# Seven half-size products in place of eight in part of the first MLP layer, in the last two tiles of a retention and MLP kernel

## The chip, the cores and the metric

The kernel runs on one core of a Trainium2 chip. The metric is the device time of one execution in microseconds (us). The engines of the core are named as in the profile: PE (TensorE, matrix products), PEld (its weight loads), DVE (VectorE), ACT (ScalarE), POOL (GpSimd) and SP (SyncE, which here issues stores). Products land in PSUM, eight banks of 512 float32 values per partition; the other operands lie in SBUF.

## The reference

Inputs are `q`, `k`, `v` of shape 8 x 8 x 576 x 64 (batch, heads, positions, head size), two small matrices `U` (576 x 32) and `V` (32 x 576) and two weight matrices `w_ch1` (512 x 2048) and `w_ch2` (2048 x 512). All are float32.

```
scores = scale * (q @ k^T) * Dmat          # Dmat[i, j] = gamma_h ** (i - j) for i >= j, else 0
x      = heads side by side of (scores @ v)   # 8 x 576 x 512
u      = x + (x^T @ U @ V)^T
out    = u + max(u @ w_ch1, 0) @ w_ch2
```

The change concerns `max(u @ w_ch1, 0)`, the first layer of the MLP.

## The kernel before

The 8 x 576 = 4608 rows of `u` are worked on as nine MLP tiles of 512 rows (`NT = 9`, tiles 0 to 8). The attention of a later batch is interleaved with the MLP of an earlier tile; tiles 7 and 8 have no attention beside them, since there are only eight batches. All matrix operands are bfloat16, and PE accumulates in float32.

The rows of `u` lie in a ring of 16 chunks of 128 rows, `ring["u"]`, and turned, `ring["uT"]` (128 partitions of one quarter of the 512 columns, four quarters `cc` apart). `w1_sb` holds the first weight matrix in four blocks of 128 rows, `w2_sb` the second in 16 blocks.

**First layer.** The 2048 columns of `w_ch1` are 16 row blocks of 128 of the turned result. For one block, `first(f)` runs four matmuls of 128 x 128 weights against 512 moving columns, accumulated in one PSUM bank, and `relu(f)` on ACT writes the block to `y1` in SBUF as bfloat16. From tile 2 on the blocks go in the order 0, 8, 1, 9, 2, 10 and so on, a block of the upper half of `y1` and its partner of the lower half in turn. So four blocks in a row (2, 10, 3, 11, say) form a two-by-two arrangement of halves.

**Second layer.** From tile 2 on it already runs in seven products instead of eight: `product(n, half)` takes quarters of `y1` (two halves of rows, two halves of blocks) and of `w2`, or sums of such quarters, in a scheme in which seven products of half-size matrices replace eight. Its matmuls have 256 moving columns, 112 in a tile. The sums of `y1` are made by DVE: `sum_up(a, z)` writes two 128x512 sums after each pair of blocks of both halves (`GROUPS` says after which unit), and `difference` overwrites a quarter after the last block. The parts of the result go through `after_1` to `after_7`, on ACT, DVE and POOL, to `o_sb` and are stored by SP.

**Order.** The units of a tile are 16 of the first layer and 14 of the second. The program issues them one after the other, and every engine works on its own instructions in the order in which they were issued (`Pinned` keeps that order); between engines there are semaphores, made from which part of a tile an instruction reads and writes. PSUM banks come from three pools: three banks "mm" (`ps_mm`), which the blocks of the first layer and the products of the second take in turn, three banks "att" and one tile of two banks "pss", which the attention uses. In tiles 7 and 8 the last two pools lie idle but for two "att" banks at the very end of tile 8, where `rows_apart` keeps the last product's two halves apart so that the first can be stored sooner.

The loop over the tiles in the kernel before is `for j in range(1, NT)`; it issues a tile's units with the attention steps that are due between them. The buffers `k_sets`, `v_sets` (three of each) and `q_raw` (two) hold the inputs of the batches and are no longer read once the last batch's attention is over, which is during tile 6.

Of the kernel before, what the change touches and what calls it, by code (L numbers as in the profile page):

```python
# [8 lines left out]
FP32 = mybir.dt.float32  # L9
BF16 = mybir.dt.bfloat16  # L10
AF = mybir.ActivationFunctionType
ALU = mybir.AluOpType
# [55 lines left out]
def kernel(  # L68
# [12 lines left out]
    pe = Pinned(tc, nc.tensor)  # L81
    dve = Pinned(tc, nc.vector)
    act = Pinned(tc, nc.scalar)
# [6 lines left out]
    R = moe_U.shape[1]  # L90
    P = 128
# [4 lines left out]
    NF = dff // P  # L96
# [5 lines left out]
    NT = B * S // 512  # L102
# [19 lines left out]
    CH = 64  # L122
# [12 lines left out]
    ps_mm = ctx.enter_context(tc.tile_pool(name="ps_mm", bufs=3, space=bass.MemoryType.PSUM))  # L135
    banks = {}
# [6 lines left out]
    q_raw = [consts.tile([P, NR_COLS], BF16, name=f"q_all{i}") for i in range(NQ)]  # L143
# [61 lines left out]
    w1_sb = consts.tile([P, NCC, dff], BF16, name="w1_sb")  # L205
# [343 lines left out]
    def mix_turn_by_dma(a, n):  # L549
# [363 lines left out]

    GROUPS = {4: (0, 2), 8: (2, 4), 12: (4, 6), 15: (6, 8)}

    def sums_of_w2(part):

        f = slice(part * HF // 2, (part + 1) * HF // 2)
        (b11, b12), (b21, b22) = (
            [w2_sb[:, fh * HF:(fh + 1) * HF, q * HD:(q + 1) * HD][:, f, :] for q in range(2)]  # L920
            for fh in range(2)
        )
        t3, t2, t4 = (w2_sums[:, i, f, :] for i in range(3))
        for to, x, y, op in (
            (t3, b22, b12, ALU.subtract), (t2, t3, b11, ALU.add), (t4, b21, t2, ALU.subtract),
        ):
            dve.tensor_tensor(out=to, in0=x, in1=y, op=op)

    def last_sum_of_w2(part):
        f = slice(part * HF // 2, (part + 1) * HF // 2)  # L930
        x = w2_sb[:, 0:HF, HD:dm][:, f, :]
        dve.tensor_tensor(out=x, in0=x, in1=w2_sb[:, 0:HF, 0:HD][:, f, :], op=ALU.subtract)

    def mlp_units(j):
        held = {}
# [65 lines left out]
        def sum_up(a, z):  # L1001

            f = slice(a, z)
            s1, s2 = (y1_sums[:, i, f, :] for i in range(2))
            dve.tensor_tensor(
                out=s1, in0=quarter(1, 0)[:, f, :], in1=quarter(1, 1)[:, f, :], op=ALU.add
            )
            dve.tensor_tensor(out=s2, in0=s1, in1=quarter(0, 0)[:, f, :], op=ALU.subtract)

        def difference(a, z):  # L1010
            f = slice(a, z)
            x = quarter(1, 0)[:, f, :]
            dve.tensor_tensor(out=x, in0=quarter(0, 0)[:, f, :], in1=x, op=ALU.subtract)
# [78 lines left out]
        def product(n, half):  # L1092
            bank, fresh, left, right, after = products[n]
            if bank not in held and rows_apart(bank):
                held[bank] = [
                    banks["one"].tile([P, 2, HD], FP32, tag="att", name="ps_y2") for _ in range(2)
                ]
            if bank not in held:
                held[bank] = ps_mm.tile([P, 2, HD], FP32, tag="mm", name="ps_y2")
            apart = rows_apart(bank)  # L1100
            for f in range(HF):
                pe.matmul(
                    bank_rows(bank, half), left()[:, f, half * P:(half + 1) * P],
                    right()[:, f, :], start=(fresh and (apart or half == 0) and f == 0),
                    stop=(f == HF - 1), skip_group_check=True,
                )
            if j == NT - 1 and after is after_3:
                after_3_rows(half)
            elif half == 1 and after:
                after()  # L1110

        def unit(n, alone=True):

            i, part = divmod(n - NF, 4)
            if n < NF:
                first(order[n])
            elif sums:
                product(*divmod(n - NF, 2))
            else:
                second(i, part)  # L1120
            if alone and n < NF:
                relu(order[n])
                if sums and n in GROUPS:
# [7 lines left out]
        steps = {"y": ahead, "R": relu, "M": lambda n: unit(n, False), "O": add_and_store}  # L1131
        return [lambda n=n: unit(n) for n in range(NF + (14 if sums else 16))], steps


# [141 lines left out]
    for h in range(H):  # L1276
# [6 lines left out]
        out=ident, in_=ident, compare_op=ALU.not_equal, fill=1.0, base=0,  # L1283
# [13 lines left out]
    for i in range(2):  # L1297
# [7 lines left out]
        out=maskbin, in_=maskbin, compare_op=ALU.is_ge, fill=0.0, base=0,  # L1305
# [27 lines left out]
    for h in range(H):  # L1333
        dve.tensor_scalar(
            out=masks[:, h, :, :], in0=mask64, scalar1=float(gammas[h] ** -CH), scalar2=None,
            op0=ALU.mult,
# [6 lines left out]
            tc.tile_pool(name="ps_" + name, bufs=n, space=bass.MemoryType.PSUM))  # L1343


    for j in range(1, NT):
# [12 lines left out]
        if j == 2:  # L1359
            steps += [(at, 3, lambda i=i: last_sum_of_w2(i)) for i, at in enumerate((2, 3))]  # L1360
        if 1 < j and j + 2 < B:
            wait_for_turns(j)
            load_for_turns(j + 2)
            if j + 3 < B:
                clear_pads(j + 3)
        if j + 2 < B:
            at = 22 if j == 1 else 20
            steps += [(at + h, 4, lambda h=h: scale_head(j + 2, h)) for h in range(H)]
        steps.sort(key=lambda s: s[:2])
        for n, unit in enumerate(units1 if j == 1 else mlp_units(j)[0]):  # L1370
            while steps and steps[0][0] <= n:
                steps.pop(0)[2]()
            if j > 1 or n >= 3:
                unit()
        for s in steps:
            s[2]()

# [28 lines left out]
```

## Time and profile before

| what | value |
|---|---|
| time, three runs | 313.93, 315.33, 315.69 us, median 315.33 us |
| the profiled execution's own time | 315.51 us |
| span of the profiled execution | 313.8 us |
| PE busy | 305.6 us (97%) |
| DVE busy | 229.0 us (73%) |
| ACT busy | 166.8 us (53%) |
| POOL busy | 131.3 us (42%) |

The span runs from the first to the last instruction; the execution's own time is longer by what lies around it. A busy share is an average over stages. The part of the span that matters here is its last 56 us: tile 7's first layer from about 258 us, its second from about 272, tile 8's from about 284 and 298. Each row of a timeline has a start, a duration, the engine, the operation, its output and inputs, a shape and a count; in square brackets stands how long the engine had been idle before, and what ended that. PSUM tiles of both layers are called `ps_y`, the first layer's result `y_t`, the sums of it `y_sums`, the sums of `w2` `kv_runs`, the parts of the output `o_sb`.

### The profile page before, as it was taken

How to read it: one execution, taken by the hardware profiler on the slowest of the kernel's cores; microseconds unless marked ns; L12 is line 12 of the kernel's file. 1: busy time of each engine (PE TensorE's matmuls, PEld its weight loads, DVE VectorE, ACT ScalarE, POOL GpSimd, SP SyncE). 2: the span in 40 equal slices, each digit the busy share in tenths (PEclk: the TensorE clock that was granted, in tenths of full speed). 3: DMA queues.
4: the chain of work that ended last, by engine and by line, in shares of the span. 5: the costliest groups of instructions: out<-in, count | busy, mean ns of one | idle time of the engine just before them, and what ended most of it. 6: DMA issues, size and time to landing. Idle time of an engine off the chain costs nothing.

```text
span 313.8 us, 9434 instructions
## 1 busy us (share of the span) xinstructions
PE 305.6 (97%) x3937; PEld 190.9 (61%) x3952; DVE 229.0 (73%) x562; ACT 166.8 (53%) x346; POOL 131.3 (42%) x171
## 2 busy tenths in 40 slices
PE   8799999999999999999999999999999999999995
PEld 3575446745544557855784578457845784685484
DVE  6776818877988997899688968996799772352245
ACT  7556605447725775377437745774377406604610
POOL 8492258849302952259439612961200120040040
PEclk9979999999999999999999999999999999999999
DMA  7999999999995999799999994999910052002003
GB/s 117 193 182 198 204 212 145 170 184 133 173 123 162 158 113 146 118 157 148 154 210 162 143 148 119 178 139 118 212 56 4 3 131 86 2 33 102 0 2 135
DMA packets 154523, 40.58 MB, mean 129 GB/s; under 512 B 139088, under 2 KB 153456, under 8 KB 154480
## 3 DMA queue, kind: packets, MB, share of 16 engines
q0 software_dynamic: 91344, 17.09, 71.7%
q1 hardware_dynamic: 63136, 22.88, 40.9%
q8 instruction: 31, 0.51, 0.7%
q14 instruction: 12, 0.10, 0.1%
HBM read 36.85 MB, written 9.44 MB: 147 GB/s over the span
## 4 chain that ended last, share of the span: by engine, by line
PE 84%; DVE 7%; DMA 4%; issue 2%; SPq 1%; ACT 0%; POOL 0%; DVEq 0%; POOLq 0%
PE ps_y L25 69%; PE xh L25 5%; PE ps_b L25 4%; DMA given<-in_v_dram 2%; DMA kv_runs<-in_v_dram 2%; PE sc L25 2%; SPq L25 1%; PE pss L25 1%; DVE u_t L25 1%; PE ps_h L25 1%; PE ps_at L25 1%; DVE v_all L25 1%; DVE S L25 1%; DVE V_sb L25 1%; DVE qT_all L25 1%
## 5 line engine op out<-in xcount | busy, mean ns | idle before, releaser
L25 PE MATMUL ps_y<-uT_t,w_sb 128*128 128x512 bf16 x576 | 130.3, 379 | 0.2
L25 ACT ACTIVATE y_t<-ps_y 128x512 bf16<-128x512 f32 x144 | 85.6, 597 | 59.6 <-PE ps_y L25 58.5
L25 PEld LDWEIGHTS <-w_sb 128*128 128x128 bf16 x576 | 54.4, 98 | 61.5 <-issue 0.4
L25 POOL TENSOR_TENSOR o_sb<-o_sb,u_t 128x512 f32<-128x512 f32 x21 | 23.9, 1152 | 104.8 <-DVE o_sb L25 100.3
L25 PEld LDWEIGHTS <-y_t 128*128 128x128 bf16 x576 | 55.2, 98 | 18.9
L25 PE MATMUL ps_y<-w_sb,y_t 128*128 128x256 bf16 (+1 forms) x345 | 56.4, 310 | 0.5 <-issue 0.2
L25 DVE SCALAR_TENSOR_TENSOR S<-S,keep,pss 128x64 bf16<-128x64 bf16 x168 | 47.0, 280 | 6.0 <-ACT S L25 0.9
L25 DVE TENSOR_TENSOR o_sb<-ps_y,o_sb 128x512 f32<-128x512 f32 (+1 forms) x37 | 24.4, 662 | 26.6 <-PE ps_y L25 12.8
L25 DVE TENSOR_TENSOR ret<-sc,qsrow 128x640 bf16<-128x640 f32 x48 | 39.2, 819 | 2.5 <-PE sc L25 2.2
L25 PEld LDWEIGHTS <-y_sums 128*128 128x128 bf16 x336 | 32.0, 98 | 5.2 <-issue 0.5
L25 POOL DMA_DIRECT2D k_all<-in_k_dram x36 | 30.1, 853 | 8.2 <-DMA w_sb<-in_moe_w_ch_dram 8.2
L25 POOL DMA_DIRECT2D q_all<-in_q_dram x37 | 29.3, 801 | 5.5 <-DMA w_sb<-in_moe_w_ch_dram 4.2
L25 ACT ACTIVATE v_all<-v_all,vs 128x320 bf16<-128x320 bf16 x40 | 18.7, 548 | 22.1 <-DMA v_all<-in_v_dram 20.8
L25 DVE TENSOR_TENSOR y_sums<-y_t 128x512 bf16<-128x512 bf16 x28 | 11.8, 420 | 22.1 <-ACT y_t L25 22.1
L25 POOL DMA_DIRECT2D v_all<-in_v_dram x31 | 26.5, 918 | 2.4 <-DMA k_all<-in_k_dram 1.6
L25 PE MATMUL ps_y<-w_sb,y_sums 128*128 128x256 bf16 x224 | 27.4, 273 | 0.1
L25 PE MATMUL ps_y<-kv_runs,y_t 128*128 128x256 bf16 x224 | 26.9, 273 | 0.2
L25 ACT ACTIVATE x_t<-xh,xs 128x320 bf16<-128x320 f32 x48 | 22.7, 523 | 7.4 <-PE xh L25 5.8
L25 DVE TENSOR_TENSOR u_t<-ps_h,x_t 128x512 bf16<-128x512 f32 (+2 forms) x39 | 22.4, 629 | 2.5 <-PE ps_h L25 2.3
L25 POOL COPY landed<-uT_t 128x4 bf16<-128x4 bf16 (+3 forms) x5 | 0.9, 188 | 38.4 <-DMA uT_t<-u_t 38.4
L25 PE MATMUL ps_y<-kv_runs,y_sums 128*128 128x256 bf16 x112 | 14.1, 273 | 0.3 <-issue 0.3
L25 PEld LDWEIGHTS <-ret 128*128 128x128 bf16 (+1 forms) x320 | 11.8, 98 | 2.5 <-issue 0.2
(133 smaller groups left out, 297.0 us busy)
## 6 DMA issues: line engine op xcount, KB each, us to landing
out_dram<-o_sb SPq DMA_DIRECT2D x35, 256.0 KB, 2.6
w_sb<-in_moe_w_ch_dram POOLq DMA_DIRECT2D x8, 512.0 KB, 12.1
v_all<-in_v_dram POOLq DMA_DIRECT2D x25, 128.0 KB, 10.8
k_all<-in_k_dram POOLq DMA_DIRECT2D x24, 128.0 KB, 6.3
q_all<-in_q_dram POOLq DMA_DIRECT2D x20, 128.0 KB, 4.8
q_all<-in_q_dram POOLq DMA_DIRECT2D x12, 144.0 KB, 6.0
given<-in_v_dram SPq DMA_DIRECT2D x8, 128.0 KB, 5.5
kv_runs<-in_v_dram SPq DMA_DIRECT2D x3, 256.0 KB, 6.0
```

Source lines behind the costliest of these rows:

```text
L25: return self._tc.keep_in_program_order(call(*args, **kwargs))
```

## The change

The loop over tiles ends before tile 7, and a new function `last_tiles` issues tiles 7 and 8 with an order written out by hand.

In each, the first layer's four groups of four blocks are treated in two ways. The first (blocks 0, 8, 1, 9) and the last (6, 14, 7, 15) stay as they are. The second (group 1: blocks 2, 10, 3, 11) and the third (group 2: 4, 12, 5, 13) are computed in the same seven-product scheme as the second layer. The halves are those of the 512 columns of `u` that are summed over (`c` = 0, 1), of the blocks (lower, upper) and of the 512 rows of the tile (`t` = 0, 1). One product `seventh(n, g)` is four matmuls of 128 x 128 weights against 256 moving columns. Seven products make 28 such matmuls for a group, where the plain group has 16 of 512 columns.

The scheme needs four sums of quarters of `w1` (`sum_of_w1`, over the columns of both groups, 128x1024 each, once) and four of quarters of `u` for each tile (`sum_of_u`, 128x512 each), all on DVE. They lie in buffers that the attention no longer uses: `w1_sums` in `k_sets` and `v_sets` 2 and 0, `u_sums` in those of number 1. The sums for tile 7 and of `w1` are issued ahead of tile 7, those for tile 8 in tile 7's second layer after unit `NF + 11`.

Products 1, 6, 7 and 4 accumulate in one "mm" bank, in that order, and ACT copies the state of the bank after products 1, 6 and 7 to `shares` (float32, in the `q_raw` buffers), each copy before the next product is added. Products 5 and 3 accumulate in an "att" bank, product 2 has a "pss" bank. The four 128x512 parts of the result are: the bank after product 4, by ACT's relu; and three that DVE makes in `finish`, each with one addition of a bank and a share and one maximum with zero in place.

The sums `sum_up` for the second layer come later than before: (0, 2) after product 7 of group 1, (2, 4) after product 7 of group 2, (4, 6) after its product 3, and (6, 8) after the last block as before.

```
+        for units, steps in tiles:
+            seventh, sum_up = steps["seventh"], steps["sum_up"]
+            for n in range(3):
+                units[n]()
+            seventh(1, 1)
+            units[3]()
+            for n, g in ((6, 1), (2, 1), (5, 1), (7, 1)):
+                seventh(n, g)
+            sum_up(0, 2)
+            for n, g in ((1, 2), (2, 2), (4, 1), (6, 2), (5, 2), (3, 1), (7, 2)):
+                seventh(n, g)
+            sum_up(2, 4)
+            for n, x in zip(range(12, NF), (4, 3, None, None)):
+                units[n]()
+                if x:
+                    seventh(x, 2)
+                if x == 3:
+                    sum_up(4, 6)
+            for n in range(NF, NF + 14):
+                units[n]()
+                if n == NF + 11 and steps is tiles[0][1]:
+                    for i in range(4):
+                        tiles[1][1]["sum_of_u"](i)
```

```
+        def sum_of_u(n):
+            (b11, b12), (b21, b22) = ([u_quarter(i, t) for t in range(2)] for i in range(2))
...
+            to, x, y = ((t1, b12, b11), (t2, b22, t1), (t3, b22, b12), (t4, b21, t2))[n]
+            dve.tensor_tensor(out=to, in0=x, in1=y, op=ALU.subtract)
+
+        def seventh(n, g):
...
+            bank, left, right = {
+                1: ("a", w(0, 0), u(0, 0)), 6: ("a", summed(1), u_sum(1)),
+                7: ("a", summed(2), u_sum(2)), 4: ("a", w(1, 1), u_sum(3)),
+                5: ("c", summed(0), u_sum(0)), 3: ("c", summed(3), u(1, 1)),
+                2: ("d", w(0, 1), u(1, 0)),
+            }[n]
+            fresh = n in (1, 5, 2)
...
+            for i in range(2):
+                for c in range(2):
+                    pe.matmul(
+                        ps[:, i, :], left(c)[:, (2 * g + i) * P:(2 * g + i + 1) * P], right(c),
+                        start=(fresh and i == 0 and c == 0), stop=(c == 1),
+                        skip_group_check=True,
+                    )
+
+            def finish(i, fh, share):
+                y = quarter(i, fh)[:, f, :]
+                dve.tensor_tensor(out=y, in0=ps, in1=kept[:, share], op=ALU.add)
+                dve.tensor_scalar(out=y, in0=y, scalar1=0.0, scalar2=None, op0=ALU.max)
+
+            if n in (1, 6, 7):
+                act.copy(out=kept[:, (1, 6, 7).index(n)], in_=ps)
...
+            if n in (5, 7) and done >= {5, 7}:
+                ps = held["L", g, "c"]
+                finish(1, 1, 2)
+            elif n == 4:
+                act.activation(out=quarter(0, 1)[:, f, :], in_=ps, func=AF.Relu)
+            elif n == 2:
+                finish(0, 0, 0)
+            elif n == 3:
+                finish(1, 0, 1)
```

More of the change, by code (lines that the diff above doesn't have):

```diff
@@ L914, with flat, w1_quarter, sum_of_w1 @@
     GROUPS = {4: (0, 2), 8: (2, 4), 12: (4, 6), 15: (6, 8)}
+    def flat(x):
+        return x.rearrange("p c h d -> p (c h d)")
+    w1_sums = [
+        flat(x)[:, 0:2 * HF * P].rearrange("p (c f) -> p c f", c=2)
+        for x in (k_sets[2], v_sets[2], k_sets[0], v_sets[0])
+    ]
+    u_sums = [
+        flat(x)[:, 0:8 * 2 * P].rearrange("p (i c t) -> p i c t", i=4, c=2)
+        for x in (k_sets[1], v_sets[1])
+    ]
+    shares = [
+        x.bitcast(FP32)[:, 0:3 * 512].rearrange("p (n f t) -> p n f t", n=3, f=2) for x in q_raw
+    ]
+    def w1_quarter(i, c):
+        return w1_sb[:, 2 * c:2 * c + 2, i * HF * P:(i + 1) * HF * P]
+    def sum_of_w1(n, a, z):
+        f = slice(a * P, z * P)
+        (a11, a12), (a21, a22) = ([w1_quarter(i, c)[:, :, f] for c in range(2)] for i in range(2))
+        s1, s2, s3, s4 = (x[:, :, f] for x in w1_sums)
+        to, x, y, op = (
+            (s1, a21, a22, ALU.add), (s2, s1, a11, ALU.subtract),
+            (s3, a11, a21, ALU.subtract), (s4, a12, s2, ALU.subtract),
+        )[n]
+        dve.tensor_tensor(out=to, in0=x, in1=y, op=op)
     def sums_of_w2(part):
@@ L1122, in unit @@
                 relu(order[n])
-                if sums and n in GROUPS:
+                if sums and n in GROUPS and (j < NT - 2 or n == NF - 1):
                     sum_up(*GROUPS[n])
@@ L1129, in unit, with u_quarter @@
                 add_and_store(i)
-        steps = {"y": ahead, "R": relu, "M": lambda n: unit(n, False), "O": add_and_store}
+        def u_quarter(i, t):
+            return ring["uT"][:, own + 2 * t:own + 2 * t + 2, 2 * i:2 * i + 2, :]
+        def sum_of_u(n):
+            (b11, b12), (b21, b22) = ([u_quarter(i, t) for t in range(2)] for i in range(2))
+            t1, t2, t3, t4 = (
+                u_sums[j % 2][:, i].rearrange("p c (h t) -> p h c t", h=2) for i in range(4)
+            )
+            to, x, y = ((t1, b12, b11), (t2, b22, t1), (t3, b22, b12), (t4, b21, t2))[n]
+            dve.tensor_tensor(out=to, in0=x, in1=y, op=ALU.subtract)
@@ new lines, in seventh, with w, summed, u @@
+        def seventh(n, g):
+            f = slice(2 * g, 2 * g + 2)
+            kept = shares[g % 2]
+            def w(i, c):
+                return lambda x: w1_quarter(i, c)[:, x]
+            def summed(i):
+                return lambda x: w1_sums[i][:, x]
+            def u(i, t):
+                return lambda x: u_quarter(i, t)[:, :, x, :]
+            def u_sum(i):
+                return lambda x: u_sums[j % 2][:, i, x, :]
+            bank, left, right = {
[5 more added lines that the diff above has]
+            fresh = n in (1, 5, 2)
+            if n == 1:
+                held["L", g, "a"] = ps_mm.tile([P, 2, 2 * P], FP32, tag="mm", name="ps_y1")
+            elif n == 5:
+                held["L", g, "c"] = banks["one"].tile(
+                    [P, 2, 2 * P], FP32, tag="att", name="ps_y1")
+            elif n == 2:
+                if "two" not in held:
+                    held["two"] = banks["two"].tile([P, 2, 8, CH], FP32, tag="pss", name="ps_y1")
+                held["L", g, "d"] = held["two"][:, g % 2].rearrange("p (f x) t -> p f (x t)", f=2)
+            ps = held["L", g, bank]
+            for i in range(2):
[4 more added lines that the diff above has]
+                        skip_group_check=True,
+                    )
+            def finish(i, fh, share):
[4 more added lines that the diff above has]
+                act.copy(out=kept[:, (1, 6, 7).index(n)], in_=ps)
+            done = held.setdefault(("L", g), set())
+            done.add(n)
+            if n in (5, 7) and done >= {5, 7}:
[3 more added lines that the diff above has]
+                act.activation(out=quarter(0, 1)[:, f, :], in_=ps, func=AF.Relu)
+            elif n == 2:
+                finish(0, 0, 0)
+            elif n == 3:
+                finish(1, 0, 1)
@@ L1132, in mlp_units @@
+        steps = {
+            "y": ahead, "R": relu, "M": lambda n: unit(n, False), "O": add_and_store,
+            "sum_of_u": sum_of_u, "seventh": seventh, "sum_up": sum_up,
+        }
         return [lambda n=n: unit(n) for n in range(NF + (14 if sums else 16))], steps
@@ L1343, with last_tiles @@
             tc.tile_pool(name="ps_" + name, bufs=n, space=bass.MemoryType.PSUM))
-    for j in range(1, NT):
+    def last_tiles():
+        tiles = [mlp_units(j) for j in (NT - 2, NT - 1)]
+        for i in range(4):
+            steps = [lambda: tiles[0][1]["sum_of_u"](i), lambda: sum_of_w1(i, 2, 6)]
+            for step in steps if i < 2 else steps[::-1]:
+                step()
+        for units, steps in tiles:
[19 more added lines that the diff above has]
+                if n == NF + 11 and steps is tiles[0][1]:
+                    for i in range(4):
+                        tiles[1][1]["sum_of_u"](i)
+    for j in range(1, NT - 2):
         if j == 1:
@@ L1376 @@
             s[2]()
+    last_tiles()
 _INS = ['q', 'k', 'v', 'moe_U', 'moe_V', 'moe_w_ch1', 'moe_w_ch2']
```

## The prediction

> **What bounds the kernel now.** I read the page first (busy shares, chain), then the end of the chain of waits, then the tail in windows, then its timeline, row by row.
>
> ```profile
> span 313.8 us, 9434 instructions
> PE 305.6 (97%) x3937; PEld 190.9 (61%) x3952; DVE 229.0 (73%) x562; ACT 166.8 (53%) x346; POOL 131.3 (42%) x171
> PE 84%; DVE 7%; DMA 4%; issue 2%; SPq 1%; ACT 0%; POOL 0%; DVEq 0%; POOLq 0%
> ...
> 250.19 60.12 PE ps_y L25 x424
> 310.33 0.42 DVE o_sb L25
> ```
>
> The last 60.12 us before the final addition are one unbroken piece of TensorE (PE) work on `ps_y`, and the changed stages lie in it. Nothing else sets the end there, so what PE saves comes off the span one for one, and what PE waits goes on.
>
> ```profile
> 257.94:271.86 13.92, 13.92 (x67) 6.37 (x65) 3.24 (x7) 8.96 (x15) 0.00 (x0) 1.00 0.21 74
> 271.86:284.00 12.14, 12.14 (x113) 10.89 (x112) 6.55 (x10) 1.18 (x2) 3.42 (x3) 1.00 0.12 43
> 284.00:297.90 13.90, 13.90 (x67) 6.33 (x65) 3.24 (x7) 8.96 (x15) 0.00 (x0) 1.00 0.11 39
> 297.90:310.30 12.40, 12.39 (x113) 10.86 (x111) 7.04 (x12) 1.18 (x2) 3.42 (x3) 1.00 0.13 45
> ```
>
> Columns: PE, weight loads, VectorE (DVE), ScalarE (ACT), GpSimd (POOL), granted clock. The rows are first layer and second layer of tile 7, then of tile 8. In the first layers PE is full at clock 1.00, DVE has 3.24 of some 13.9 us of work and ACT 8.96. So DVE has room, and the question is whether its new work comes in time.
>
> ```profile
> 258.05 13.98 PE L25 MATMUL ps_y<-uT_t,w_sb 128*128 128x512 bf16 x64
> 258.32 0.69 DVE L25 TENSOR_TENSOR o_sb<-ps_y,o_sb 128x512 f32<-128x512 f32 x1 [1.07 <-PE ps_y L25]
> 260.84 0.60 ACT L25 ACTIVATE y_t<-ps_y 128x512 bf16<-128x512 f32 x1 [0.27 <-PE ps_y L25]
> 271.86 1.91 PE L25 MATMUL ps_y<-w_sb,y_t 128*128 128x256 bf16 x16
> 272.06 0.60 ACT L25 ACTIVATE y_t<-ps_y 128x512 bf16<-128x512 f32 x1 [0.27 <-PE ps_y L25]
> 272.69 0.42 DVE L25 TENSOR_TENSOR y_sums<-y_t 128x512 bf16<-128x512 bf16 x1 [2.57 <-ACT y_t L25]
> 273.15 0.42 DVE L25 TENSOR_TENSOR y_sums<-y_sums,y_t 128x512 bf16<-128x512 bf16 x1
> 273.49 1.28 DVE L25 TENSOR_TENSOR y_t<-y_t 128x1024 bf16<-128x1024 bf16 x2
> 273.81 0.58 ACT L25 COPY o_sb<-ps_y 128x512 f32<-128x512 f32 x1 [1.15 <-PE ps_y L25]
> 282.60 0.69 DVE L25 TENSOR_TENSOR o_sb<-ps_y,o_sb 128x512 f32<-128x512 f32 x1 [0.34 <-issue]
> 284.09 13.98 PE L25 MATMUL ps_y<-uT_t,w_sb 128*128 128x512 bf16 x64
> 284.36 0.69 DVE L25 TENSOR_TENSOR o_sb<-ps_y,o_sb 128x512 f32<-128x512 f32 x1 [1.07 <-PE ps_y L25]
> ```
>
> ```profile
> L25 PE MATMUL ps_y<-uT_t,w_sb x128: 379/379/379, 258.0 to 297.7; 128*128 128x512 bf16 x128
> L25 PE MATMUL ps_y<-w_sb,y_t x64: 272/272/273, 271.9 to 306.5; 128*128 128x256 bf16 x64
> ```
>
> A matmul's record includes its drain: the 64 of 512 columns start every (13.98 - 0.379)/63 = 0.216 us, the 16 of 256 columns every (1.91 - 0.272)/15 = 0.109 us. The drain is 0.163 us (0.379 - 0.216, 0.272 - 0.109). ACT starts 0.03 after a matmul's end (272.03 to 272.06), DVE 0.03 after ACT's (272.66 to 272.69).
>
> **The PE saving.** A group of four row blocks is now 16 matmuls of 512 columns, 16 x 0.216 = 3.45 us. Seven half-size products are 28 of 256 columns, 28 x 0.109 = 3.06 us. Two groups in two tiles: 4 x 0.397 = 1.59 us with the unrounded steps (0.2159, 0.1092). That is the ceiling, 0.50% of the time. Everything else can only take from it.
>
> **The sums of weights and of u.** Four 128x1024 and four 128x512 subtractions or additions go to DVE ahead of tile 7, four of the latter inside its second layer for tile 8.
>
> ```profile
> L25 DVE TENSOR_TENSOR kv_runs<-w_sb 128x1024 bf16<-128x1024 bf16 x2 | 1.4, 689 | 0.0
> L25 DVE TENSOR_TENSOR y_sums<-y_sums,y_t 128x512 bf16<-128x512 bf16 x28 | 11.9, 425 | 1.0
> L25 DVE TENSOR_TENSOR o_sb<-ps_y,o_sb 128x512 f32<-128x512 f32 x33 | 22.8, 691 | 26.0 <-PE ps_y L25 12.2 <-ACT at_diag L25 7.4 <-issue 6.1
> L25 DVE TENSOR_TENSOR u_t<-ps_b,x_t 128x512 bf16<-128x512 f32 x4 | 2.4, 659 | 0.0
> L25 DVE CAST uT_t<-ps_b 128x512 bf16<-128x512 f32 x3 | 2.1, 692 | 1.6 <-PE ps_b L25 1.6
> L25 DVE COPY V_sb<-V_sb 32x576 bf16<-32x576 bf16 x7 | 1.9, 298 | 0.1
> ```
>
> I count from PE's start of tile 7, 258.05. DVE is free at 0.96 (258.32 + 0.69). The first four sums take 2 x 0.69 + 2 x 0.43 = 2.23, done by 3.2 to 3.35; product 6 needs them at 3.89: hidden, slack 0.55. The other four end at 5.4 to 5.8; products 7 (5.23, which needs the first two of them, by 4.5) and 4 (6.54) do not wait. For tile 8 the sums follow the addition at 282.60, end about 285.1, and push the addition now at 284.36 to 285.1 to 285.8. Its bank is wanted by the third row block of tile 8, at 284.09 + 8 x 0.216 = 285.82: hidden, with the cover nearly used up, 0 to 0.07 us if it goes. The store behind that addition leaves 0.7 later, and SP has no other store until tile 8's.
>
> **The waits through ACT.** Products 1, 6, 7, 4 share a bank, and each but the first must wait until ACT has copied out the state before it (P1 to P6, P6 to P7, P7 to P4). The loop from the last matmul's issue slot is drain 0.163 + 0.03 + copy 0.585 + 0.04 = 0.82 us. The 0.04 is this:
>
> ```profile
> 167.66 0.29 DVE S L25
> 167.95 0.04 issue
> 167.99 0.22 PE xh L25 x2
> ...
> 165.62 1.61 ACT L25 ACTIVATE y_t<-ps_y 128x512 bf16<-128x512 f32 x3
> ```
>
> The same hand-over from ACT to PE I take at 0.04 too. The last row gives ACT's pitch back to back, (1.61 - 0.60)/2 = 0.51. What lies between on PE is two products, 8 x 0.109 = 0.87, or one plain block, 0.86: 0.05 more than the loop, if ACT is free. It is not always. Placing the slots (plain 0.863, product 0.437): P6 of the first product group could start at 3.89, but ACT's relu of the third block (starts 2.79) puts the copy at 3.30 to 3.88, so P6 starts at 3.92. P7 at 5.23 finds its copy done at 5.21. The second group's P1 copy starts behind the first's P7 copy, at 6.37, so P6 goes at 6.99 for 6.98; its P7 at 8.30 for 8.30. Without overlap on ACT (0.60 instead of 0.51) four of these slip 0.09 each. Bounds 0.05 to 0.4 us per tile; I take 0.2. ACT itself does what it did: four copies or relus in place of four relus.
>
> **DVE's additions and maxima.** Each group has three additions from PSUM (bounds 0.659 to 0.692, above) each followed by a maximum in place, which no row shows. Its price lies between the 0.298 of a 576-element copy in bf16 and the 0.692 of a copy out of PSUM; I take 0.30, as bf16 in SBUF with one input is nearest to the first. From 273.15 against 272.69 + 0.42, a dependent DVE instruction waits 0.04; the pair at 273.49 takes 1.28, 0.64 each, so an independent one starts some 0.04 early. An addition and its maximum thus take 0.69 + 0.04 + 0.30 - 0.04 = 0.98 to 1.02; a pair of `sum_up` 0.85 to 0.9. The last product that waits for DVE is P3 of the second group: its bank must first be read by the addition behind P7. DVE's order up to there: P7 copy of the first group lands 6.45; addition and maximum to 7.47; `sum_up(0, 2)` to 8.33; P2's pair of group two to 9.31; P3's of group one to 10.29; the addition to 10.98. P3 could go at 10.90 and goes at 11.02. With no overlap at all it is 11.25. I take 0.2 us per tile (bounds 0.1 to 0.4, in tile 7 0.6 when the late sums push the chain).
>
> By the Trainium skill, "VectorE: DVE Perf Modes", section "The DRAIN you can't avoid", the next DVE instruction does not start until the pipe is empty; the pair at 273.49 disagrees by 0.09 us. By that rule P3 would go at 11.25, and the change would gain 0.3 us less.
>
> The bank of products 1, 6, 7, 4 is one of the three that the plain blocks turn through, and is held some 4 us instead of under 2. The tightest reuse is the plain block 7, which takes the bank of the second group's P4: its relu ends at 10.04 + 0.19 + 0.60 = 10.8, the block starts at 11.46. Hidden, slack 0.6.
>
> Late next: `sum_up(4, 6)` and `(6, 8)` then end about 15.0, and the second layer wants their last rows at 13.2 + 1.75 + 0.65 = 15.6 (before: done 273.57, wanted 274.27). Covered.
>
> **The sum.** Per tile -0.79 + 0.2 + 0.2 = -0.4; two tiles -0.8. The profiled execution took 315.51 (span 313.8 and 1.7 around it): 314.7. It lies 0.18 above the median 315.33, against which it is 314.5. I write 314.6.
>
> **Rivals.**
> *No wait at all*: 315.51 - 1.59 = 313.9. For it: the loops nearly fit. Against: three places are already full by the rows.
> *The waits eat the gain*: seven PE slots per tile hang on ACT or DVE; 0.06 us more at each is 0.4 per tile, and the time is 315.5. For it:
>
> ```profile
> 48.60 0.69 ACT L25 COPY kvT<-ps_b 128x640 bf16<-128x640 bf16 x1 [0.81 <-PE ps_b L25]
> 48.63 1.04 PE L25 MATMUL ps_y<-w_sb,y_t 128*128 128x512 bf16 x4
> 49.59 0.44 PEld L25 LDWEIGHTS <-kvT 64*128 64x128 bf16 x10 [0.42 <-ACT kvT L25]
> ```
>
> PE came 0.30 after that copy's end, and 0.10 after its own four matmuls' slots (48.63 + 4 x 0.216 = 49.49). Against: there the shape of the array also changes.
> *Slower, DVE is the bound*: the maximum costs 0.69. P3 of the second group then waits 0.2 + 3 x 0.39 = 1.37; per tile -0.79 + 0.2 + 1.37 = +0.78; 315.51 + 1.56 = 317.1. It decides from where the maximum takes over 0.30 + 0.39/3 = 0.43 us. Against: the 0.298 row.
> *The clock falls*:
>
> ```profile
> 8.00:16.00 8.00, 6.31 (x180) 4.86 (x179) 6.28 (x14) 4.53 (x11) 3.97 (x8) 1.00 1.19 187
> 16.00:24.00 8.00, 7.89 (x139) 5.99 (x135) 5.68 (x11) 4.48 (x12) 7.74 (x11) 0.79 1.14 188
> ```
>
> Early on PE idled 1.7 of 8 us, and the clock was 0.79 in the next 8: 1.7 us lost. Once in each tile: 314.7 + 3.4 = 318.1. Against: the waits above sum to 0.4 of 13 us. The Trainium skill, "TensorE: Matmul & The Clock Gate", section "A second HAM failure mode: psum-queue depth-cycling", says that micro-idles between matmul groups can make the clock oscillate; that is this rival. The unbroken tail at 1.00 does not test it.
>
> **How the numbers follow.** Forecast 0.57, no wait 0.08, waits eat the gain 0.18, DVE bound 0.13, clock 0.04. A change of 0.5% (1.58 us) is about what a measurement of this kernel can tell from none; the three runs spread over 0.56%. As the ceiling is 0.50%, "faster" needs the no-wait case or a lucky draw of the forecast: 0.18. "Slower" is the DVE case, most of it, and the clock: 0.14. The rest, 0.68, is "same". The range is 313.3 (no wait, less the scatter) to 316.9 (most of the DVE case); outside lie the clock, the worst of DVE and a lucky tenth. Within the forecast alone, from the bounds of the two waits (0.15 to 0.8 per tile): 314.2 to 315.5.
>
> **What would show it.** First layers of tiles 7 and 8 from 13.81 to about 13.4 us each, second layers unchanged; PE gaps of under 0.15 us ahead of P6 and about 0.1 to 0.3 ahead of the second P3; the maximum at 0.30; granted clock 1.00. I am wrong if the maximum takes over 0.43, if gaps ahead of the ACT-fed products exceed 0.1 each, or if the third block of tile 8 starts late.

## The result, and the profile after

| what | before | after |
|---|---|---|
| time, median of 22 runs each | 315.22 us | 313.75 us |
| lowest and highest run | 313.78, 319.62 us | 312.33, 316.19 us |
| the profiled execution's own time | 315.51 us | 314.12 us |
| its span | 313.8 us | 312.4 us |

The ratio is 0.9951, with a 95% interval of 0.9929 to 0.9972: faster by 0.3 to 0.7%. This ratio and those below leave out a few executions in which the device was in a slower state. In microseconds the ratio is 315.22 x 0.0049 = 1.5, nearly all of the 1.59 that the PE slots could give. The forecast was 314.6, a gain of 0.8 to 0.9.

The page of the changed kernel: the span and the busy shares, and the end of the chain of waits.

```profile
span 312.4 us, 9587 instructions
PE 303.1 (97%) x3985; PEld 194.6 (62%) x4000; DVE 244.9 (78%) x598; ACT 165.7 (53%) x346; POOL 131.5 (42%) x171
...
250.31 58.60 PE ps_y L25 x472
308.93 0.42 DVE o_sb L25
```

The last piece of PE work is still unbroken and is 60.12 - 58.60 = 1.52 us shorter. DVE has 15.9 us more work (244.9 for 229.0), and none of it shows up in that chain. The four stages of the tail, in windows (columns: PE, weight loads, DVE, ACT, POOL, granted clock, DMA share, GB/s):

```profile
258.17:271.22 13.05, 13.05 (x91) 8.60 (x88) 11.73 (x26) 8.35 (x15) 0.00 (x0) 1.00 0.22 77
271.22:283.45 12.23, 12.23 (x114) 10.96 (x113) 7.95 (x15) 1.18 (x2) 3.43 (x3) 1.00 0.13 43
283.45:296.50 13.05, 13.05 (x91) 8.60 (x88) 8.55 (x20) 8.36 (x15) 0.00 (x0) 1.00 0.12 41
296.50:308.93 12.43, 12.39 (x113) 10.86 (x111) 7.67 (x15) 1.18 (x2) 3.43 (x3) 1.00 0.13 45
```

Both first layers take 13.05 us. Before, the first matmul of tile 7's first layer started at 258.05 and that of its second at 271.86, which is 13.81; so each fell by 0.76, of the 0.79 that the slots allow. PE is busy through the whole window. DVE went from 3.24 to 11.73 of the 13 us in tile 7, ACT stayed about where it was, and the clock is 1.00. The second layers kept their time.

How the three engines hand over to each other is in the timeline of tile 7's first layer:

```profile
258.17 4.05 PE L25 MATMUL ps_y<-uT_t,w_sb 128*128 128x512 bf16 x20
260.31 0.68 DVE L25 TENSOR_TENSOR v_all<-k_all,w_sb 128x1024 bf16<-128x1024 bf16 x1
261.45 0.58 ACT L25 COPY q_all<-ps_y 128x512 f32<-128x512 f32 x1
262.08 0.60 PE L25 MATMUL ps_y<-v_all,v_all 128*128 128x256 bf16 x4
262.46 0.42 DVE L25 TENSOR_TENSOR v_all<-uT_t,v_all 128x512 bf16<-128x512 bf16 x1
263.21 0.69 DVE L25 TENSOR_TENSOR y_t<-ps_y,q_all 128x512 bf16<-128x512 f32 x1 [0.33 <-ACT y_t L25]
...
266.38 0.68 DVE L25 TENSOR_TENSOR y_t<-ps_y,q_all 128x512 bf16<-128x512 f32 x1
267.09 0.29 DVE L25 TENSOR_SCALAR y_t<-y_t 128x512 bf16<-128x512 bf16 x1
267.30 0.68 DVE L25 TENSOR_TENSOR y_t<-ps_y,q_all 128x512 bf16<-128x512 f32 x1
268.23 0.68 DVE L25 TENSOR_TENSOR y_t<-ps_y,q_all 128x512 bf16<-128x512 f32 x1
269.06 0.60 PE L25 MATMUL ps_y<-uT_t,v_all 128*128 128x256 bf16 x4
```

The sums of `u` and `w1` are the DVE rows into `v_all` and `k_all`, the shares are `q_all`. Three places matter. Product 6 of group 1 starts at 262.08; the copy that it waits for (261.45) ended at 262.03, so the loop through ACT is closed with nothing to spare, and PE loses 0.02. The pair of addition and maximum on DVE takes 0.92 from start to start (266.38 to 267.30, and 0.93 to 268.23). The last addition ahead of product 3 of group 2 ends at 268.91, and the product goes in its own slot at 269.06: 0.15 later, which after a hand-over of 0.04 leaves 0.11 to spare. No PE row of the stage has an idle time in brackets.

### The profile page after: what moved, and what is told of

Read it like the earlier page. It is cut to its first block, busy times and chain, and to the rows that moved or that the text cites. A ratio compares the mean times of both kernels' runs of the same rounds, so it can differ in the third digit from the quotient of the medians.

```text
span 312.4 us, 9587 instructions
## 1 busy us (share of the span) xinstructions
PE 303.1 (97%) x3985; PEld 194.6 (62%) x4000; DVE 244.9 (78%) x598; ACT 165.7 (53%) x346; POOL 131.5 (42%) x171
## 5 line engine op out<-in xcount | busy, mean ns | idle before, releaser
L25 PE MATMUL ps_y<-uT_t,w_sb 128*128 128x512 bf16 (+1 forms) x544 | 121.8, 373 | 0.4 <-ACT y_t L25 0.2
L25 ACT ACTIVATE y_t<-ps_y 128x512 bf16<-128x512 f32 x132 | 78.2, 597 | 56.9 <-PE ps_y L25 55.2
L25 PEld LDWEIGHTS <-w_sb 128*128 128x128 bf16 x560 | 52.9, 98 | 54.1 <-issue 0.9
L25 PEld LDWEIGHTS <-k_all 64*64 64x64 bf16 (+2 forms) x596 | 13.2, 109 | 4.2 <-issue 3.1
```

Source lines behind the costliest of these rows:

```text
L25: return self._tc.keep_in_program_order(call(*args, **kwargs))
```

## The experiments

Two theories were put against each other. T: the gain is the PE slots alone, and every wait is hidden by the amount that the placed slots and the rows of the profile give. R: the waits are hidden by another margin than that, larger or smaller, or what counts is something else (the clock, the hand-over between engines, a bank). The runs take parts away, use up one cover at a time, and at the end use the margins that are left. Stage times below are tile 7's first layer, tile 7's second, tile 8's first, from the first PE start of a stage to that of the next. Where PE waits behind matmuls, the bracket counts from the end of their drain, so the slots lost are the bracket and 0.16 more (the 0.163 of the prediction).

**One tile plain** (tile 7 as before, tile 8 as changed):

```
+            if steps is tiles[0][1]:
+                for n in range(NF):
+                    units[n]()
+                    if n in GROUPS and n < NF - 1:
+                        sum_up(*GROUPS[n])
...
+                continue
```

> Tile 7 plain again, tile 8 as in the changed kernel. If the gain is the PE slots of the removed products, tile 7's first layer takes 13.8 us as before and tile 8's 13.05, and the time is 0.76 us above that of the changed kernel. If part of the gain came from elsewhere (the new order of issue, the earlier end of the loop over tiles), tile 7's first layer stays under 13.8 or other stages differ too.

The windows of this run, first layer of tile 7 and of tile 8:

```profile
257.02:270.83 13.81, 13.81 (x66) 6.24 (x64) 5.73 (x11) 8.96 (x15) 0.00 (x0) 1.00 0.21 72
283.06:296.11 13.05, 13.05 (x90) 8.59 (x88) 8.55 (x20) 8.36 (x15) 0.00 (x0) 1.00 0.12 41
```

Within one execution the plain tile takes 13.81 and the changed one 13.05: tile 8 gains its 0.76 whether tile 7 is changed or not. The run took 313.76 us, no more than the kernel with both tiles changed, because its tile 7 started 1.15 us earlier than that one's (257.02 for 258.17); the last section comes back to that.

**Product 2's matmuls twice**, so that a group has eight products' worth of slots:

```
-            for i in range(2):
+            for i in list(range(2)) * (2 if n == 2 else 1):
```

> Product 2 of each group is run twice, the second time over the first, so a group has eight half-size products again. If all of the gain is the eighth product that is saved, the first layers take 13.05 + 2 x 0.437 = 13.92 us, a little above the 13.81 of the plain ones, and the time is 0.2 us above that of the kernel before. If the half-size form itself brings or costs something, they differ from 13.92.

```profile
255.32:269.25 13.93, 13.93 (x99) 9.37 (x96) 12.03 (x27) 8.36 (x15) 0.00 (x0) 1.00 0.21 72
281.48:295.40 13.92, 13.92 (x98) 9.39 (x96) 8.85 (x21) 8.36 (x15) 0.00 (x0) 1.00 0.11 38
```

Eight more matmuls in a tile cost 0.88 and 0.87 us, 8 x 0.109 = 0.87. A PE slot in these stages counts one for one. That is the mechanism of the change, run backwards. The single time, 313.02 us, is below the changed kernel's median although the tail is 1.75 longer: tile 7 began at 255.32.

**The maximum twice** (the same `tensor_scalar` issued two times):

```
                 dve.tensor_scalar(out=y, in0=y, scalar1=0.0, scalar2=None, op0=ALU.max)
+                dve.tensor_scalar(out=y, in0=y, scalar1=0.0, scalar2=None, op0=ALU.max)
```

> The maximum in each of the three finishes is issued twice (the second changes nothing). If VectorE's chain up to the second group's product 3 has the 0.1 us of slack that the trace of the changed kernel shows, three more maxima of 0.29 plus 0.04 for the dependence make that product 0.9 us late: first layers 13.05 to about 13.9 us in both tiles, the whole gain gone. If VectorE has more room than that, the first layers stay at 13.05 to 13.2.

The window of tile 7's first layer, and its timeline at product 3 of group 2:

```profile
258.44:272.39 13.95, 13.22 (x90) 8.57 (x88) 12.81 (x30) 8.35 (x15) 0.00 (x0) 1.00 0.21 72
```

```profile
269.49 0.68 DVE L25 TENSOR_TENSOR y_t<-ps_y,q_all 128x512 bf16<-128x512 f32 x1
270.21 0.62 DVE L25 TENSOR_SCALAR y_t<-y_t 128x512 bf16<-128x512 bf16 x2
270.23 0.60 PE L25 MATMUL ps_y<-uT_t,v_all 128*128 128x256 bf16 x4 [0.73 <-DVE y_t L25]
```

Two maxima take 0.62, 0.33 more than one. Four such double maxima lie ahead of the addition that frees product 3's bank. The first costs nothing: in the changed kernel DVE stands idle for 0.41 us behind it, until ACT's copy for the next addition (264.64) is there. The other three count: 3 x 0.33 = 0.99, of which 0.11 is to spare, leaves 0.88; the slot lost is 0.73 + 0.16 = 0.89. The whole loss is at this one place, the one that the prediction named as the last product to wait for DVE. With 0.33 more per maximum the stage is 0.14 above the kernel before.

**No plain block between products 1 and 6:**

```
-            seventh(1, 1)
             units[3]()
+            seventh(1, 1)
```

> The plain block that lies between products 1 and 6 of the first group is issued ahead of product 1, so nothing covers ScalarE's copy. If the loop is drain 0.163 + 0.03 + copy 0.585 + 0.04 us, a little more as the copy queues behind the block's relu, product 6 waits 0.85 us and the first layers take 13.9. If the hand-over from ScalarE to TensorE costs 0.3 as the one row of the kernel before suggested, the wait is 1.1 and they take 14.15 or more.

```profile
261.12 0.58 ACT L25 COPY q_all<-ps_y 128x512 f32<-128x512 f32 x1
261.75 0.60 PE L25 MATMUL ps_y<-v_all,v_all 128*128 128x256 bf16 x4 [0.72 <-ACT q_all L25]
```

Product 6 follows the copy's end (261.70) by 0.05. The stages were 13.92, 12.23, 13.91, 0.86 to 0.87 more than changed: the loop from product 1 through ACT, uncovered. So the rival that put 0.30 from ACT to PE is out; the 0.04 taken from DVE to PE holds for ACT to 0.01.

**The sums twice** (each of the eight sums ahead of tile 7 issued two times; tile 8's own are not touched):

```
             for step in steps if i < 2 else steps[::-1]:
                 step()
+                step()
```

> Each sum of w1 and of u is made twice in tile 7's part of VectorE's work (those of u for tile 8 once, as before). If the cover of the sums is what the trace of the changed kernel shows (the first four done 1.1 us before product 6 wants them, VectorE idle a further 0.3 us before the first finish), product 6 of tile 7 waits 1.0 us, the chain of finishes starts about 3.8 us late, product 3 of the second group waits, and tile 7's first layer goes from 13.05 to 16.2 to 16.4 us; tile 8's stays 13.05. If the sums are covered with more room, tile 7's first layer stays under 15.

```profile
256.57:273.63 17.06, 13.54 (x90) 8.45 (x88) 16.20 (x34) 8.47 (x15) 0.00 (x0) 1.00 0.17 59
```

```profile
261.83 0.61 PE L25 MATMUL ps_y<-v_all,v_all 128*128 128x256 bf16 x4 [1.21 <-DVE v_all L25]
263.96 0.61 PE L25 MATMUL ps_y<-v_all,k_all 128*128 128x256 bf16 x4 [0.64 <-DVE v_all L25]
265.94 0.68 DVE L25 TENSOR_TENSOR y_t<-ps_y,q_all 128x512 bf16<-128x512 f32 x1
266.68 0.60 PE L25 MATMUL ps_y<-uT_t,w_sb 128*128 128x256 bf16 x4 [1.67 <-DVE y_t L25]
```

The expectation missed here: it had 16.2 to 16.4 for the stage, 1.0 for the wait at product 6 and a wait at product 3 of group 2. The first two waits, at products 6 and 7 of group 1, are those that late sums must give. Product 3 of group 2, at 271.47, shows no wait. The third wait, 1.67 + 0.16 = 1.83, was not in any theory: product 2 of group 2 waits until DVE has finished product 2 of group 1 (265.94 + 0.68 = 266.62). They do not share a bank. But both banks are slices of one tile, `held["two"]`, and the wait is made as if the tile were one thing. The description of the kernel says that semaphores follow the part of a tile that is read or written; the two halves of this tile were not told apart. The three waits sum to 1.37 + 0.80 + 1.83 = 4.00, and the stage grew by 4.01. In the changed kernel the same wait is there and covered: the addition at 263.21 ends at 263.90, and product 2 of group 2 comes at 264.26.

**The sums twice, product 2 of group 1 in an "att" bank of its own:**

```
+            elif n == 2 and g == 1:
+                held["L", g, "d"] = banks["one"].tile(
+                    [P, 2, 2 * P], FP32, tag="att", name="ps_y1")
```

> The kernel with the sums ahead of tile 7 made twice, but with an att bank for product 2 of the first group instead of half of the pss tile. If product 2 of the second group waited there only because the two banks are one tile, that wait (1.8 us) goes; TensorE then waits about 1.0 us at product 3 of the first group and 0.5 at that of the second, for additions that are as late as before, and tile 7's first layer is 16.7 to 16.8 us instead of 17.06. If it waited for anything else, the wait stays.

```profile
264.14 1.04 PE L25 MATMUL ps_y<-uT_t,w_sb 128*128 128x256 bf16 x8
265.82 0.61 PE L25 MATMUL ps_y<-v_all,w_sb 128*128 128x256 bf16 x4 [0.64 <-DVE v_all L25]
270.92 0.60 PE L25 MATMUL ps_y<-uT_t,v_all 128*128 128x256 bf16 x4 [0.38 <-DVE y_t L25]
```

The wait at product 2 of group 2 is gone (it is in the run of eight matmuls from 264.14), so the shared tile was its cause. The stage is 16.77 instead of 17.06, only 0.29 less, as most of the DVE work was still late and PE met it at the next places: product 4, which waits for the last sum of `u`, and product 3 of group 2 (0.80 and 0.54 with the drain). Product 3 of group 1 lost another 0.20 (it comes 0.64 after the product before it, for a slot of 0.44). The length was foreseen, and product 3 of group 2; product 4 as a place was not, and product 3 of group 1 had been put at 1.0.

**Three groups in tile 8** (group 0 too in seven products there; the `w1` sums of its columns, four of 128x512, issued in tile 7's second layer at unit `NF + 3`):

```
+            if steps is tiles[1][1]:
+                for n, g in (
+                    (1, 0), (2, 0), (5, 0), (6, 0), (1, 1), (2, 1), (7, 0), (6, 1), (5, 1),
+                    (4, 0), (7, 1), (1, 2), (3, 0), (2, 2), (4, 1), (6, 2), (5, 2), (3, 1),
+                    (7, 2),
+                ):
+                    seventh(n, g)
...
+                if n == NF + 3 and steps is tiles[0][1]:
+                    for i in range(4):
+                        sum_of_w1(i, 0, 2)
```

> In tile 8 alone the first group of blocks is computed in seven half-size products too; its sums of w1 are made in tile 7's second layer. If only PE slots bind and VectorE still keeps up, tile 8's first layer goes from 13.05 to 13.05 - 0.40 = 12.66 us and the time falls by 0.4 against the changed kernel. If VectorE, with nine finishes instead of six, is the bound, product 3 of the last such group waits 0.4 us or more and nothing is gained.

Stages 13.06, 12.93, 12.93; ratio 0.9974 (0.9949 to 0.9999). By its slots tile 8's first layer should lose another 0.40 (12.65). It fell by 0.12, and tile 7's second layer grew by 0.70. The timeline of that second layer:

```profile
273.20 0.42 DVE L25 TENSOR_TENSOR k_all<-w_sb 128x512 bf16<-128x512 bf16 x1
273.37 3.86 POOL L25 TENSOR_TENSOR o_sb<-o_sb,u_t 128x512 f32<-128x512 f32 x3 [22.43 <-DVE o_sb L25]
273.65 1.26 DVE L25 TENSOR_TENSOR v_all<-k_all,w_sb 128x512 bf16<-128x512 bf16 x1
274.84 1.37 DVE L25 TENSOR_TENSOR k_all<-w_sb 128x512 bf16<-128x512 bf16 x1
276.13 1.37 DVE L25 TENSOR_TENSOR v_all<-w_sb,v_all 128x512 bf16<-128x512 bf16 x1
...
278.16 1.91 PE L25 MATMUL ps_y<-kv_runs,y_t 128*128 128x256 bf16 x16 [0.41 <-DVE o_sb L25]
```

The same subtraction takes 0.42 alone and 1.26 to 1.37 while POOL adds to `o_sb`. POOL's three took 3.86, for 3.51 in the changed kernel. The addition that reads out a bank stands behind the sums on DVE, and PE waited for that bank. The Trainium skill, "SBUF — State Buffer", section "Who interferes with whom", says that a DVE instruction with two inputs in SBUF contends with a GpSimd instruction that reads SBUF. The trace agrees, and puts a number to it: three times the duration.

**Three groups in both tiles** (the `w1` sums of three groups' columns, 128x1536 each, in the second layers of tiles 5 and 6; a similar order of products):

```
+            if n == NF and j in (5, 6):
+                for i in range(2):
+                    sum_of_w1(2 * (j - 5) + i, 0, 6)
```

> Three groups of four in seven products in both tiles; the sums of w1 are made in the second layers of tiles 5 and 6, in a pause of 2 us that VectorE has there. If only PE slots bind, both first layers go to 12.66 us, and the time falls by 0.8 us against the changed kernel, if the four sums (0.95 us each) fit that pause. If VectorE binds, the first layers stay above 13, or tiles 5 and 6 grow by what the sums take.

Stages 15.63, 12.22, 14.61; ratio 1.0106 (1.0062 to 1.0150): slower. PE has fewer slots and waits for more than it saved. Timeline of tile 7's first layer:

```profile
259.57 0.68 DVE L25 TENSOR_TENSOR y_t<-ps_y,q_all 128x512 bf16<-128x512 f32 x1
260.31 0.60 PE L25 MATMUL ps_y<-uT_t,w_sb 128*128 128x256 bf16 x4 [1.60 <-DVE y_t L25]
...
267.43 0.58 ACT L25 COPY q_all<-ps_y 128x512 f32<-128x512 f32 x1 [1.41 <-DVE y_t L25]
268.07 0.60 PE L25 MATMUL ps_y<-v_all,k_all 128*128 128x256 bf16 x4 [0.93 <-ACT q_all L25]
```

The first wait is the shared two-bank tile again: product 2 of group 1 stands behind the finish of product 2 of group 0, which stands on DVE behind the sums of `u`. The second is a buffer: groups 0 and 2 take the same share buffer (`g % 2`), so ACT may not write group 2's copy until DVE has read group 0's, and product 7 waits for ACT. The `w1` sums in tiles 5 and 6 cost nothing: from the start of their second layers to the next first layer it is 13.89 and 13.38 us, and 13.88 and 13.39 in the changed kernel.

**Three groups in tile 8, mended.** A bank of its own for product 2 of group 1 in tile 8, a buffer of its own for group 0's share of product 6, product 3 of group 1 ahead of product 5 of group 2, and the `w1` sums away from POOL's additions:

```
+            if g == 0:
+                kept[1] = share_0
...
+            elif n == 2 and j == NT - 1 and g == 1:
+                held["L", g, "d"] = banks["one"].tile(
+                    [P, 2, 2 * P], FP32, tag="att", name="ps_y1")
...
+                if n == NF and steps is tiles[0][1]:
+                    for i in range(2):
+                        sum_of_w1(i, 0, 2)
...
+                    for i in range(2, 4):
+                        sum_of_w1(i, 0, 2)
```

> Again three groups in seven products in tile 8 alone, with the three costs of the earlier try taken away: two of the four added sums of w1 are made before GpSimd's additions in tile 7's second layer and two after them, product 2 of the second of the three groups has an att bank of its own, and the share of product 6 of the first group has its own buffer. If those were the costs, the four sums take 0.42 us each, tile 7's second layer is 12.23 us again (12.93 in the earlier try), tile 8's first layer is 12.66 to 12.8 (13.05 in the changed kernel), and the time is 0.3 us below that of the changed kernel. If VectorE binds all the same, tile 8's first layer stays at 12.9 or more.

Two of the four `w1` sums, one early and one late, and the windows of tile 7's second and tile 8's first layer:

```profile
274.34 0.42 DVE L25 TENSOR_TENSOR v_all<-k_all,w_sb 128x512 bf16<-128x512 bf16 x1
...
284.19 0.42 DVE L25 TENSOR_TENSOR v_all<-w_sb,v_all 128x512 bf16<-128x512 bf16 x1
```

```profile
271.05:283.28 12.23, 12.23 (x114) 10.96 (x113) 8.71 (x17) 1.18 (x2) 3.42 (x3) 1.00 0.12 43
283.28:295.92 12.64, 12.64 (x102) 9.75 (x100) 11.37 (x26) 8.24 (x15) 0.00 (x0) 1.00 0.12 43
```

The sums are back at 0.42, the second layer at 12.23, and the first layer is at 12.64, which is all of the 0.40. So what three groups in tile 8 lost at first is gone with the contention, the bank, the buffer and the order together. The trace of the first try tells which of them counted in tile 8's 12.93:

```profile
289.29 0.59 ACT L25 COPY q_all<-ps_y 128x512 f32<-128x512 f32 x1
289.92 0.60 PE L25 MATMUL ps_y<-k_all,k_all 128*128 128x256 bf16 x4
```

Product 7 of group 2 (289.92) comes 0.64 after the product before it, 0.20 more than a slot, which is most of the 0.28 that was lost. It waits for the copy at 289.29, and that starts 0.12 after the end (289.17) of DVE's addition that reads group 0's share, as the copy at 267.43 did in the run with three groups in both tiles (0.11). So the buffer is the likely cause. No product 2 of that tile comes late, so there the shared bank cost nothing.

The ratio was 0.9938 (0.9910 to 0.9966). The changed kernel was timed beside it once more:

> The changed kernel itself, beside the one with three groups on the same chip: first layers of 13.05 us in both tiles, second layers 12.23, and a time 0.3 us above that of the kernel with three groups if its costs were the named ones.

Its ratio beside the same runs of the kernel before was 0.9956 (0.9919 to 0.9993), its first layers again 13.05 and 13.06. The two intervals overlap: between these two kernels the times alone decide nothing, the stages do.

**Three groups in both tiles, mended** in the same way:

```
-            elif n == 2 and j == NT - 1 and g == 1:
+            elif n == 2 and g == 1:
...
+            if n == NF and j in (5, 6):
+                for i in range(2):
+                    sum_of_w1(2 * (j - 5) + i, 0, 6)
```

> Three groups in seven products in tile 7 as well as in tile 8, with the same mending (own att bank for product 2 of the second group, own buffer for one share); the sums of w1 are made in the second layers of tiles 5 and 6, in VectorE's pause there, where they took 0.95 us each in the earlier try. If nothing else binds, tile 7's first layer is 12.66 to 12.8 us too and the time 0.7 to 0.8 us below that of the changed kernel (0.4 below the kernel with three groups in tile 8 alone). If VectorE's late start in tile 7 (it finishes tile 6 about 0.9 us into the stage, and then makes the sums of u) makes it the bound, tile 7's first layer stays at 13 or more.

```profile
256.96:269.70 12.74, 12.74 (x102) 9.74 (x100) 11.54 (x27) 8.36 (x15) 0.00 (x0) 1.00 0.23 79
269.70:281.93 12.23, 12.23 (x113) 10.96 (x112) 8.37 (x16) 1.18 (x2) 3.42 (x3) 1.00 0.13 44
281.93:294.58 12.65, 12.65 (x102) 9.74 (x100) 10.80 (x24) 8.24 (x15) 0.00 (x0) 1.00 0.12 41
```

The median was 312.28 us, the ratio 0.9899 (0.9853 to 0.9945): the lowest of all, though its interval overlaps those of the changed kernel and of three groups in tile 8. By the stages it gains 1.07 and 1.16 over the kernel before (13.81 each), of 3 x 0.397 = 1.19 a tile. The 2.23 us together are 0.7% and lie inside the interval.

## Why the prediction was right or wrong

- **The PE saving** was right: 0.397 a group, and 0.76 of 0.79 a tile came out. Eight more slots cost 0.87.
- **The waits through ACT** were taken at 0.2 us a tile; they are 0.02 to 0.03. Here the working was right and was not used. The placed slots gave product 6 at 3.92 after the start of the tile, and it came at 3.91 (262.08 - 258.17); the other two places that were called full lost nothing that a row shows. The hand-over of 0.04 from ACT to PE, borrowed from DVE to PE, measured 0.04 to 0.05. The 0.2 was a middle between bounds whose upper end (0.4) no row supported.
- **The maximum** was taken at 0.30 and took 0.29. But the price from which it would make the kernel slower, 0.43, was too low. It stood on the padded waits: with the 0.11 to spare at product 3 and the gain of 0.76, it is 0.29 + (0.76 + 0.11)/3 = 0.58. The run with two maxima (0.62) was at +0.14 a tile, just past it.
- **DVE's pitch** is the step of the sum that was read wrongly. The passage "the pair at 273.49 takes 1.28, 0.64 each, so an independent one starts some 0.04 early" splits the pair in halves. One of 128x1024 lasts 0.68 (the row at 260.31), so the second starts at 1.28 - 0.68 = 0.60, an overlap of 0.08. The prediction had the row for it (689 ns for one of 128x1024) and states the 0.09 itself one paragraph on, but its sum goes by the 0.04. An addition with its maximum takes 0.92, not 0.98. The addition ahead of product 3 ended at 10.74 instead of 10.98, the product went at 10.89 as scheduled, and the 0.2 a tile for DVE was zero. Here too the sum took more than its working gave (11.02 for 10.90, which is 0.12).
- **The late sums of tile 7** were all made at 4.71 (262.46 + 0.42 - 258.17), not 5.4 to 5.8, so the 0.6 for "the late sums push the chain" did not come. That the sums can hurt when they double was right in kind; the shared two-bank tile, which the prediction did not see, made it worse.
- **Tile 8's bank**, "the cover nearly used up", has 0.47 us left. The same overlap is the reason:

```profile
281.96 0.69 DVE L25 TENSOR_TENSOR o_sb<-ps_y,o_sb 128x512 f32<-128x512 f32 x1 [0.34 <-issue]
...
283.69 0.42 DVE L25 TENSOR_TENSOR k_all<-uT_t,k_all 128x512 bf16<-128x512 bf16 x1
284.03 0.68 DVE L25 TENSOR_TENSOR o_sb<-ps_y,o_sb 128x512 f32<-128x512 f32 x1
```

  The addition ends at 284.71; the third block is due at 283.45 + 8 x 0.216 = 285.18.
- **The rule on the drain.** The Trainium skill, "VectorE: DVE Perf Modes", section "The DRAIN you can't avoid", would have had product 3 at 11.25 by the prediction's estimate (added up again from its rows, no overlap gives about 11.2). It went at 10.89. That section also says that an instruction which is not held starts earlier; the overlap of 0.08 fits that.
- **The clock** stayed at 1.00 in all the stages of the tail, also where PE stood still for up to 1.7 us inside a stage of 13 to 17 us, and in the stage behind. So the rival of a falling clock is out for gaps of this size in the tail. The rule on micro-idles (the Trainium skill, "TensorE: Matmul & The Clock Gate", section "A second HAM failure mode: psum-queue depth-cycling") did not show in these stages. The rival's own row was weaker than it looked: the clock early on does not simply follow PE's idle time. Between 8 and 16 us PE idled 1.64 us in the run without the block between, and the clock of the next 8 us was 1.00; in the run with two maxima it idled 0.77, and the clock fell to 0.79.
- **The forecast as a whole.** The mechanism was right and two terms were over-sized: 0.4 a tile for waits instead of 0.03. What happened is the no-wait rival (313.9), which was given 0.08 because "three places are already full by the rows". A place that is full by the rows, but not over, loses nothing; that argument was for it, not against. The gain was nearly twice the forecast, and two of the signs that were named did not come: first layers of 13.4 us, and a gap of 0.1 to 0.3 ahead of the second product 3. That 313.75 lies in the range of 313.3 to 316.9 speaks for the width of the range, whose lower end was this rival, and not for the two waits. The change was also easier to tell from none than the prediction held: with 22 runs of each kernel the interval is 0.2% to either side, not 0.5%.

## What to carry to other kernels

When a stage is bound by PE, count the matmul slots, place every other engine's instructions against them from rows, and put the result into the sum as it comes out: worked-out waits of 0.05 and 0.12 a tile, each padded to 0.2, were most of the error here. Two instructions back to back have a pitch of their total less one duration, not half the total. Before more work is laid beside such a stage, look for what ties independent products together (a tile of two banks, a buffer in rotation) and for two-input DVE work beside GpSimd; with these out of the way a third group gained almost all of its slots too.

## What the runs showed of the hardware that was not expected

A DVE subtraction of two bfloat16 operands in SBUF went from 0.42 to 1.26 and 1.37 us beside GpSimd's additions, which themselves went from 3.50 to 3.86 for three.

The part of the program ahead of tile 7 varies by more than the change is worth. The instructions there are the same in the three runs named here, yet tile 7 began at 255.32 in the run with eight products, at 258.17 in the first profile of the changed kernel and at 259.85 in the second:

```profile
259.85:272.90 13.05, 13.05 (x90) 8.57 (x88) 11.72 (x26) 8.36 (x15) 0.00 (x0) 1.00 0.22 77
```

The stages after it agree to 0.01 from one execution to the next. The granted clock is likely part of the difference: in the second profile of the changed kernel it was 0.91 from 8 to 16 us and 0.66 from 16 to 24 us, which is 3.4 us of full clock lost, and 1.00 there in the other two. As those two are still 2.85 apart, it isn't all of it, and the rest stays open. So a single time here says little, and a difference of 0.4 us has to be read from the stages.
